# An attention and MoE kernel on one core: where the last stores stand, which engine makes widths and biases, and a new instruction order

## The chip, the cores and the metric

The kernel runs on one core of a Trainium2 chip. A core has engines with queues of their own: TensorE (PE, matmuls; PEld is its weight load), VectorE (DVE), ScalarE (ACT), GpSimd (POOL) and SyncE (SP), which here issues all DMAs. Each engine takes its instructions in order and waits on semaphores for the others. The metric is device microseconds (us) of one execution; the time of a kernel is the median of its runs.

## The reference

Attention over 4 batches, 8 heads, 768 positions and 64 columns, in which a query sees only keys of its own hash bucket, and then a gated two-matrix layer ("MoE") on the result. Cut to what matters:

```python
q_bucket = sum(((q @ proj) > 0) * 2**arange(6));  k_bucket = the same of k
scores = where(q_bucket[..., None] == k_bucket[:, :, None], q @ k.T / 8, -1e9)
attn = exp(scores - max(scores));  attn = attn / (sum(attn) + 1e-9)
x = (attn @ v), heads side by side: 3072 x 512
out = ((x @ w_a) * (x @ w_b)) @ w_out        # 512 -> 1536 -> 512, all float32
```

## The kernel before

Float32 operands are split into a high and a low float16 part, and a product is three float16 matmuls (high-high, high-low, low-high). The kernel is a list of some 3,600 small steps; `op(engine, duration, function, key, reads, writes, alt=...)` adds one. A step may name other engines in `alt`. The list ORDER, found by a search and written out as numbers, fixes the order of all steps: `issue` goes through it, an entry x above 9999 takes alternative x // 10000 of step x % 10000, and a negative entry -n puts n filler matmuls (`warm`) on PE. Every engine's queue follows ORDER.

Work is tiled by batch b, chunk c of 256 positions (three a batch) and half (two pairs of heads), so there are 24 units of 8 score tiles each, 192 in all, numbered u in a unit. The first two units use float32 for their attention (`by_pe`).

- Head: `kprep`, `qprep` and `vload` load q, k and v (SP), find a scale (`magnitude`, `scale_of`: a matmul of PE spreads a maximum, DVE makes the power of two), split (`split`, `vsplit`: high part on ACT, DVE or POOL, low part by `low` on DVE) and transpose. `proj_parts` scales the projection `pj`; its maximum goes through the matmul `ps_proj`. `w_group` and `wo_group` split the weights in the same way.
- A score tile, `qtile`: PE makes the scores `s` (one of two banks of PSUM), DVE the row maximum `mx` (L1164), then `width` (L1173, DVE), the 128x1 factor of the exponential, and `bias` (L1180 on ACT, or L1186 on DVE), then ACT the exponential `e` (L1196), which frees the bank. `e` is cast to float16 (`a`, high), subtracted (`a`, low, POOL or DVE, L1219 or L1223), transposed by a DMA and multiplied with `vv` on PE (`av`, L1238).
- `moe`: per chunk, 12 slices f of the hidden size: PE `ab` (L1389), ACT `a`, DVE `g`, its high part, POOL its low part g1 (L1432), PE `o` (L1442). At the end of a chunk two tiles of 128 rows are evicted to `ob` (two buffers, tag `ob`) and stored by SP (L1510). In the very last chunk (`alone`) the second tile is evicted in two halves of its columns, one by ACT (L1471) and one by DVE (L1478), into one `ob` buffer.

In ORDER the store of tile (b 3, c 1, u 1) is step 3355. Its eviction is step 3354, whose place is some 80 entries ahead of the end; step 3355 itself is the last entry of all, behind 3614, the store of the last tile:

```python
    3604, 3600, 3605, 3606, 3607, 3608, 13610, 3611, 3612, 3613, 3614, 3355,
```

(3607 and 3608 are the last `o` matmuls of tiles 0 and 1, 13610 the eviction of tile 0 on DVE, 3611 its store, 3612 and 3613 the halves of tile 1.)

Of the kernel before, what the change touches and what calls it, by code (L numbers as in the profile page):

```python
# [12 lines left out]
F32 = mybir.dt.float32  # L13
# [3 lines left out]
AF = mybir.ActivationFunctionType  # L17
ALU = mybir.AluOpType
# [3 lines left out]
P = 128  # L22
NB, NH, S, D = 4, 8, 768, 64
# [52 lines left out]
def constants():  # L76
# [1531 lines left out]
```

## Time and profile before

| what | us |
|---|---|
| three runs | 891.8, 887.73, 893.16; median 891.8 |
| the profiled execution | 890.85 |
| its span, first to last instruction | 889.1 |
| busy in it: PE, DVE, ACT, POOL | 858.7, 634.0, 507.4, 431.1 |
| mean granted clock of PE | 0.995 of full speed |

The profile is of one execution. Busy times are those of instructions, not of waits; a busy PE isn't PE at its peak, since matmuls are pipelined. "issue" is idle time that nothing in the profile explains. A wait is put down to the semaphore that came last.

### The profile page before, as it was taken

The page shows a single profiled execution, that of the slowest core. Times are in us where ns is not written, and L with a number is a line of the kernel's source. Part 1 is how long each engine was busy: PE and PEld are TensorE (multiplying, and loading weights), DVE is VectorE, ACT ScalarE, POOL GpSimd, SP SyncE. Part 2 cuts the span into 40 slices and gives each one's busy share as a digit, 9 for nine tenths or more (in the row PEclk, how much of TensorE's full clock was granted, in tenths as well). Part 3 has the DMA queues.
Part 4 walks back from the last instruction along what each step waited for, and adds up shares of the span by engine and source line. Part 5 has one row for each costly group of instructions (what it writes and reads, how often), then busy time and mean ns, then how long its engine had stood idle before and what let it go on. Part 6 is the DMA issues. An engine that isn't in the chain of part 4 may idle for free.

```text
span 889.1 us, 22944 instructions
## 1 busy us (share of the span) xinstructions
PE 858.7 (97%) x9255; PEld 654.1 (74%) x9255; DVE 634.0 (71%) x1390; ACT 507.4 (57%) x988; POOL 431.1 (48%) x399
## 2 busy tenths in 40 slices
PE   6799999999999999999999999999999999999996
PEld 4578766777777777777777777777777777777774
DVE  6999999987867777867765675787877568653211
ACT  6899998856566555564443445544674454432211
POOL 4558886645466456655353344542256542232111
PEclk9999999999999999999999999999999999999998
DMA  9968999999999899999857768988988975644000
GB/s 324 335 129 242 189 230 205 197 179 200 201 189 171 150 170 182 191 171 193 160 114 114 122 136 155 186 159 165 207 166 153 178 121 114 94 93 84 11 3 36
DMA packets 416986, 142.60 MB, mean 160 GB/s; under 512 B 388592, under 2 KB 409200, under 8 KB 416880
## 3 DMA queue, kind: packets, MB, share of 16 engines
q1 hardware_dynamic: 416880, 141.14, 82.0%
q8 instruction: 72, 1.18, 0.6%
q14 instruction: 34, 0.28, 0.1%
HBM read 37.82 MB, written 6.29 MB: 50 GB/s over the span
## 4 chain that ended last, share of the span: by engine, by line
PE 81%; DVE 10%; DMA 4%; issue 2%; ACT 1%; POOL 1%; SPq 1%; DVEq 0%; ACTq 0%; POOLq 0%
PE ab L1389 39%; PE o L1442 19%; PE s L1150 11%; PE av L1238 9%; DVE mx L1164 2%; DVE wab L573 1%; DMA vr<-in_v_dram 1%; DVE wmx L642 1%; DMA at<-a 1%; DVE vv L855 1%; DVE a L1223 1%; DMA qTA_q<-marked 1%; ACT e L1196 1%; DMA raw_w<-in_moe_w_a_dram 1%; DMA raw_wo<-in_moe_w_out_dram 0%
## 5 line engine op out<-in xcount | busy, mean ns | idle before, releaser
L1389 PE MATMUL ab<-xT,wab 128*128 128x256 f16 x3456 | 409.4, 272 | 1.9 <-DVE g L1412 1.9
L1389 PEld LDWEIGHTS <-wab 128*128 128x128 f16 x3456 | 332.9, 98 | 59.6 <-issue 3.1
L1432 POOL TENSOR_TENSOR g<-g,g 128x256 f16<-128x256 f32 x144 | 113.0, 785 | 308.7 <-ACT g L1420 135.2
L1196 ACT ACTIVATE e<-s,bias,width 128x768 f32<-128x768 f32 x192 | 189.9, 989 | 73.3 <-DVE bias L1186 57.9
L1164 DVE TENSOR_REDUCE mx<-s 128x1 f32<-128x768 f32 x192 | 182.0, 950 | 36.0 <-PE s L1150 35.3
L1442 PE MATMUL o<-wo,g 128*128 128x512 f16 x864 | 207.6, 379 | 0.0
L1219 POOL TENSOR_TENSOR a<-e,a 128x768 f16<-128x768 f32 x102 | 169.7, 1665 | 63.2 <-DVE a L1207 24.4
L1404 ACT ACTIVATE a<-ab,wcut 128x256 f32<-128x256 f32 x144 | 67.9, 471 | 183.1 <-PE ab L1389 182.0
L1412 DVE SCALAR_TENSOR_TENSOR g<-ab,wlow,a 128x256 f32<-128x256 f32 x132 | 63.5, 481 | 136.7 <-ACT a L1404 115.6
L1442 PEld LDWEIGHTS <-g 128*128 128x128 f16 x864 | 81.8, 98 | 77.1
L1238 PEld LDWEIGHTS <-at 128*128 128x128 f16 x3168 | 110.8, 98 | 16.6 <-DMA at<-a 3.3
L1238 PE MATMUL av<-vv,at 128*128 128x64 f16 x3168 | 116.2, 193 | 0.3 <-DMA at<-a 0.2
L1150 PE MATMUL s<-kTA_k,qTA_q 128*128 128x384 f16 x384 | 93.8, 326 | 5.2 <-ACT e L1196 3.3
L1150 PE MATMUL s<-kTB_k,qTB_q 128*128 128x384 f16 x384 | 93.7, 326 | 0.0
L1223 DVE TENSOR_TENSOR a<-e,a 128x768 f16<-128x768 f32 x74 | 80.2, 1086 | 9.3 <-POOL a L1209 6.0
L1208 ACT CAST a<-e 128x768 f16<-128x768 f32 x78 | 64.3, 828 | 7.9 <-issue 4.0
L1180 ACT ACTIVATE bias<-mx,width 128x1 f32<-128x1 f32 x89 | 25.8, 291 | 55.8 <-DVE width L1173 55.6
L1150 PEld LDWEIGHTS <-qTB_q 128*128 128x128 f16 x384 | 37.5, 98 | 24.9
L1209 POOL CAST a<-e 128x768 f16<-128x768 f32 x43 | 38.9, 907 | 23.2 <-ACT e L1196 15.6
L1420 ACT CAST g<-g 128x256 f16<-128x256 f32 x73 | 29.3, 402 | 36.1 <-DVE g L1412 22.5
L1150 PEld LDWEIGHTS <-qTA_q 128*128 128x128 f16 x384 | 34.0, 98 | 20.1 <-issue 7.5
L1173 DVE TENSOR_SCALAR width<-mx,qsig_q 128x1 f32<-128x1 f32 x192 | 39.5, 209 | 3.6
(165 smaller groups left out, 800.2 us busy)
## 6 DMA issues: line engine op xcount, KB each, us to landing
rk_k<-in_k_dram SPq DMA_DIRECT2D x16, 384.0 KB, 4.3
rq_q<-in_q_dram SPq DMA_DIRECT2D x12, 512.0 KB, 4.7
vr<-in_v_dram SPq DMA_DIRECT2D x16, 384.0 KB, 4.3
raw_w<-in_moe_w_b_dram SPq DMA_DIRECT2D x12, 512.0 KB, 6.9
raw_w<-in_moe_w_a_dram SPq DMA_DIRECT2D x12, 512.0 KB, 7.7
raw_wo<-in_moe_w_out_dram SPq DMA_DIRECT2D x12, 512.0 KB, 5.2
out_dram<-ob SPq DMA_DIRECT2D x24, 256.0 KB, 3.0
at<-a SPq DMA_TRANSPOSE x176, 4.0
```

The lines of the kernel that those rows point to most:

```text
L1150: nc.tensor.matmul(ps.t[:, jj, :HALF], lhsT=x.t[:, uq, :], rhs=y.t[:, h * NT + jj * 3 : h * NT + jj * 3 + 3, :].rearrange("p t x -> p (t x)"),
L1164: lambda: nc.vector.tensor_reduce(out=mx.t[:, u : u + 1], in_=halves(ps.t), axis=AX.XY, op=ALU.max, negate=True),
L1196: lambda: nc.scalar.activation(flat2(e.t), halves(ps.t), AF.Exp, bias=bias.t[:, u : u + 1], scale=width.t[:, u : u + 1], accum_out=sm.t[:, ...
L1208: ("ACT", 0.725, lambda: nc.scalar.copy(out=a2.t[:, 0], in_=e.t), False),
L1219: lambda: nc.gpsimd.tensor_tensor(out=a2.t[:, 1], in0=e.t, in1=a2.t[:, 0], op=ALU.subtract),
L1223: lambda: nc.vector.tensor_tensor(out=a2.t[:, 1], in0=e.t, in1=a2.t[:, 0], op=ALU.subtract), True,
L1238: nc.tensor.matmul(av.t[:, u, :], lhsT=at.t[:, a + kt, :], rhs=w.t[:, h, kt, x, :], start=i == 0, stop=i == 3 * NT - 1,)
L1389: nc.tensor.matmul(pl.t[:, m, :CH], lhsT=wt(m, wi, cc, f), rhs=xt.t[:, cc // 2, xi, cc % 2 * TPC : (cc % 2 + 1) * TPC, :], start=i == 0, s ...
L1404: lambda a=a, pl=pl, gr=gr: nc.scalar.activation(a.t, pl.t[:, 0, :CH], AF.Copy, scale=wcut[:, gr : gr + 1]),
L1412: lambda a=a, g32=g32, pl=pl, cut=cut: nc.vector.scalar_tensor_tensor(out=g32.t, in0=pl.t[:, 1, :CH], scalar=cut, in1=a.t, op0=ALU.mult, o ...
L1432: lambda g=g, g32=g32: nc.gpsimd.tensor_tensor(out=g[1].t, in0=g32.t, in1=g[0].t, op=ALU.subtract),
L1442: nc.tensor.matmul(po.t[:, u, :], lhsT=g[gi].t[:, us], rhs=wo[f // 2].t[:, f % 2, wi * DM : (wi + 1) * DM], start=f % per_q == 0 and i == ...
```

## The change

1. Widths may go to POOL (`wide`), biases too (`moved`), and low parts of q and k too (`low_too`, two instructions).
2. The halves of the last tile are evicted into two buffers of the tag `e` (`end_0`, `end_1`), and each half has a store of its own.
3. ORDER is another list. In it step 3355 stands right behind its eviction; the last two `o` groups are swapped; there are 16 more fillers (144 for 128); 51 widths, 25 biases and 2 low parts take POOL; among the first DMAs the two loads of `pj` stand ahead of `ident` and of the first q load.

```diff
 ORDER = [
...
-    3604, 3600, 3605, 3606, 3607, 3608, 13610, 3611, 3612, 3613, 3614, 3355,
+    3538, 3533, 3348, 3349, 3539, 3534, 3350, 3545, 3352, 3353, 13354, 3355, 3540, 3535, 3546, 3536, 3541, 3530, 3547,
...
+    3601, 3599, 3593, 3603, 3604, 3600, 3605, 3606, 3608, 3607, 3612, 3614, 13610, 3611, 3613, 3615,
 ]
...
+        def low_too():
+            nc.gpsimd.tensor_scalar(out=x, in0=x, scalar1=sc.t, scalar2=1.0, op0=ALU.mult, op1=ALU.mult)
+            nc.gpsimd.tensor_tensor(out=part(B, lo_at), in0=x, in1=part(B, hi_at), op=ALU.subtract)
+
+        op(
+            "DVE", -0.03 + 0.073 * n, low, key, r=[raw, *rtoks, (B, "hi")], w=[(B, "lo")],
+            sbuf=True, alt=[("POOL", 0.2 + 0.2 * n, low_too, False)],
         )
...
+        def wide(eng):
+            eng.tensor_scalar(
                 out=width.t[:, col], in0=mx.t[:, col], scalar1=NONE, scalar2=sig.t[:, hp : hp + 1], op0=ALU.is_lt, op1=ALU.mult
+            )
+        op(
+            "DVE", 0.13, lambda: wide(nc.vector), key - 0.5, r=[(mx, u), (sig, half)], w=[(width, u)],
+            alt=[("POOL", 0.17, lambda: wide(nc.gpsimd), False)],
+        )
+        def moved(eng):
+            eng.tensor_scalar(
+                out=bias.t[:, col], in0=mx.t[:, col], scalar1=width.t[:, col], scalar2=top, op0=ALU.mult, op1=ALU.add
+            )
...
+            alt=[("DVE", 0.15, lambda: moved(nc.vector), False), ("POOL", 0.17, lambda: moved(nc.gpsimd), False)],
         )
...
                 if alone and u == TPC - 1:
-                    hs = [slice(0, DM // 2), slice(DM // 2, DM)]
+                    ends = [buf("e", [P, S], F32, f"end_{x}", NE) for x in range(2)]
+                    cols = [slice(x * DM // 2, (x + 1) * DM // 2) for x in range(2)]
                     op(
                         "ACT", 0.36,
...
+                            ends[0].t[:, : DM // 2], po.t[:, u, cols[0]], AF.Copy, scale=osc.t
...
+                            out=ends[1].t[:, : DM // 2], in0=po.t[:, u, cols[1]], scalar1=osc.t, scalar2=None, op0=ALU.mult
...
+                    for x in range(2):
+                        op(
+                            "SP", DMA_ISSUE,
+                            lambda u=u, x=x: nc.sync.dma_start(
+                                out=out_v[b, c * TPC + u][:, cols[x]], in_=ends[x].t[:, : DM // 2]
+                            ),
+                            ke + 4, r=[ends[x]], w=[("out", b, c, u, x)], svc=0.8,
+                        )
+                    continue
```

## Rows read from the trace of the kernel before

**Rows 1.** busy time of the engines by stretch: start:end, length, each engine, PE's clock, DMA

```profile
0.00:25.00 25.00, 15.67 (x184) 11.46 (x184) 18.02 (x51) 17.90 (x22) 10.05 (x16) 1.00 0.92 324
25.00:150.00 125.00, 113.25 (x1188) 90.75 (x1188) 118.44 (x256) 115.64 (x190) 88.85 (x66) 0.99 0.94 221
150.00:880.00 730.00, 728.26 (x7881) 551.40 (x7879) 496.32 (x1082) 373.38 (x777) 332.15 (x318) 1.00 0.81 145
```

**Rows 2.** the same view, of the tile `warm` alone: length, PE busy

```profile
0.00:150.00 150.00, 19.89 (x128) 0.99 0.93 238
```

**Rows 3.** timeline of the end: start, us, engine, line, operation, tiles, idle before it and releaser

```profile
877.48 4.05 PE L1442 MATMUL o<-wo,g 128*128 128x512 f16 x18
881.57 0.75 DVE L1492 TENSOR_SCALAR ob<-o,osc 128x512 f32<-128x512 f32 x1 [2.77 <-PE o L1442]
884.47 0.47 ACT L1471 ACTIVATE ob<-o,osc 128x256 f32<-128x256 f32 x1 [5.17 <-DMA out_dram<-ob]
884.97 0.48 DVE L1478 TENSOR_SCALAR ob<-o,osc 128x256 f32<-128x256 f32 x1 [2.65 <-ACT ob L1471]
885.48 0.81 SPq L1510 DMA_DIRECT2D out_dram<-ob  x2
```

**Rows 4.** the line of the output stores: issue time of one, first and last start, landing

```profile
L1510 SPq DMA_DIRECT2D out_dram<-ob x24: 332/876/1516, 210.7 to 885.9; - x24
DMA to landing us min/median/max: 2.0/3.0/4.2
```

**Rows 5.** the chain that ended last, at the end: start, us, what

```profile
882.35 2.01 DMA out_dram<-ob
```

**Rows 6.** groups by line and form (busy, mean ns), and the smallest POOL operation (min/median/max ns)

```profile
L1173 DVE TENSOR_SCALAR width<-mx,qsig_q 128x1 f32<-128x1 f32 x192 | 39.5, 209 | 3.6
L1186 DVE TENSOR_SCALAR bias<-mx,width 128x1 f32<-128x1 f32 x103 | 21.7, 210 | 2.3 <-DVE width L1173 0.2
L1219 POOL TENSOR_TENSOR a<-e,a 128x768 f16<-128x768 f32 x102 | 169.7, 1665 | 63.2 <-DVE a L1207 24.4 <-ACT a L1208 23.0 <-issue 8.2
L1093 POOL TENSOR_SCALAR qsig_q<-kinv,qmx_q x11: 258/265/700, 25.8 to 617.0; 128x2 f32<-128x2 f32 x11
```

**Rows 7.** who waited for whom: us in all, times, longest

```profile
ACT e L1196 <- DVE bias L1186: 57.9, 37, 4.8
PE s L1150 <- ACT e L1196: 3.3, 5, 1.2
```

**Rows 8.** timeline, the line of v's low part, and a stretch, in the head

```profile
31.86 2.98 POOL L669 TENSOR_TENSOR wab<-wab 128x1024 f16<-128x1024 f32 x1
32.78 2.88 DVE L855 SCALAR_TENSOR_TENSOR vv<-vr,vsc,vv 128x768 f16<-128x768 f32 x1
L855 DVE SCALAR_TENSOR_TENSOR vv<-vr,vsc,vv x16: 998/1010/2876, 15.7 to 664.1; 128x768 f16<-128x768 f32 x16
39.98 1.00 PE L1117 MATMUL et<-ident,e 128*128 128x128 f32 x6 [2.76 <-ACT e L1196]
42.00:44.00 2.00, 2.00 (x12) 1.75 (x11) 2.00 (x4) 1.30 (x2) 2.00 (x2) 0.50 0.75 143
```

**Rows 9.** timeline of the first 15 us

```profile
1.75 0.43 SPq L1038 DMA_DIRECT2D rq_q<-in_q_dram  x1
2.22 1.36 SPq L432 DMA_DIRECT2D pj<-in_proj_dram  x2
6.99 0.16 DVE L493 TENSOR_REDUCE pmx<-pj 128x1 f32<-128x6 f32 x1 [1.39 <-DMA pj<-in_proj_dram]
7.70 0.90 POOL L974 TENSOR_SCALAR nB_k<-rk_k,ks_k 128x768 f16<-128x768 f32 x1 [6.09 <-DVE ks_k L480]
8.75 1.00 DVE L990 SCALAR_TENSOR_TENSOR nB_k<-rk_k,ks_k,nB_k 128x768 f16<-128x768 f32 x1
9.67 1.10 DVE L502 TENSOR_SCALAR pjk<-pj,psc 128x6 f16<-128x6 f32 x1
12.88 1.42 ACT L944 COPY kTB_k<-t_k_DVE 128x1536 f16<-128x1536 f16 x1
```

More of the change, by code (lines that the diff above doesn't have):

```diff
@@ L988, in split, with low @@
         )
-        def low(eng):
-            eng.scalar_tensor_tensor(
+        def low():
+            nc.vector.scalar_tensor_tensor(
                 out=part(B, lo_at), in0=x, scalar=sc.t, in1=part(B, hi_at), op0=ALU.mult, op1=ALU.subtract
             )
-        op(
-            "DVE", -0.03 + 0.073 * n, lambda: low(nc.vector), key, r=[raw, *rtoks, (B, "hi")], w=[(B, "lo")],
-            sbuf=True,
+        def low_too():
+            nc.gpsimd.tensor_scalar(out=x, in0=x, scalar1=sc.t, scalar2=1.0, op0=ALU.mult, op1=ALU.mult)
+            nc.gpsimd.tensor_tensor(out=part(B, lo_at), in0=x, in1=part(B, hi_at), op=ALU.subtract)
+        op(
+            "DVE", -0.03 + 0.073 * n, low, key, r=[raw, *rtoks, (B, "hi")], w=[(B, "lo")],
+            sbuf=True, alt=[("POOL", 0.2 + 0.2 * n, low_too, False)],
         )
@@ L1170, in qtile @@
         col = slice(u, u + 1)
-        op(
-            "DVE", 0.13,
-            lambda: nc.vector.tensor_scalar(
-                out=width.t[:, col], in0=mx.t[:, col], scalar1=NONE, scalar2=sig.t[:, hp : hp + 1], op0=ALU.is_lt, op1=ALU.mult
-            ),
-            key - 0.5, r=[(mx, u), (sig, half)], w=[(width, u)],
-        )
+        def wide(eng):
+            eng.tensor_scalar(
+                out=width.t[:, col], in0=mx.t[:, col], scalar1=NONE, scalar2=sig.t[:, hp : hp + 1], op0=ALU.is_lt, op1=ALU.mult
+            )
+        op(
+            "DVE", 0.13, lambda: wide(nc.vector), key - 0.5, r=[(mx, u), (sig, half)], w=[(width, u)],
+            alt=[("POOL", 0.17, lambda: wide(nc.gpsimd), False)],
+        )
+        def moved(eng):
+            eng.tensor_scalar(
+                out=bias.t[:, col], in0=mx.t[:, col], scalar1=width.t[:, col], scalar2=top, op0=ALU.mult, op1=ALU.add
+            )
         op(
@@ L1183, in qtile @@
             key - 0.5, r=[(mx, u), (width, u)], w=[(bias, u)],
-            alt=[(
-                "DVE", 0.15,
-                lambda: nc.vector.tensor_scalar(
-                    out=bias.t[:, col], in0=mx.t[:, col], scalar1=width.t[:, col], scalar2=top,
-                    op0=ALU.mult, op1=ALU.add,
-                ),
-                False,
-            )],
+            alt=[("DVE", 0.15, lambda: moved(nc.vector), False), ("POOL", 0.17, lambda: moved(nc.gpsimd), False)],
         )
@@ L1467, in moe @@
                 if alone and u == TPC - 1:
-                    hs = [slice(0, DM // 2), slice(DM // 2, DM)]
+                    ends = [buf("e", [P, S], F32, f"end_{x}", NE) for x in range(2)]
+                    cols = [slice(x * DM // 2, (x + 1) * DM // 2) for x in range(2)]
                     op(
                         "ACT", 0.36,
-                        lambda u=u, osc=osc, po=po, h=hs[0]: nc.scalar.activation(
-                            ob[u].t[:, h], po.t[:, u, h], AF.Copy, scale=osc.t
+                        lambda u=u, osc=osc, po=po: nc.scalar.activation(
+                            ends[0].t[:, : DM // 2], po.t[:, u, cols[0]], AF.Copy, scale=osc.t
                         ),
-                        ke - 8, r=[(po, u), osc], w=[(ob[u], 0)],
+                        ke - 8, r=[(po, u), osc], w=[ends[0]],
                     )
@@ L1477, in moe @@
                         "DVE", 0.34,
-                        lambda u=u, osc=osc, po=po, h=hs[1]: nc.vector.tensor_scalar(
-                            out=ob[u].t[:, h], in0=po.t[:, u, h], scalar1=osc.t, scalar2=None, op0=ALU.mult
+                        lambda u=u, osc=osc, po=po: nc.vector.tensor_scalar(
+                            out=ends[1].t[:, : DM // 2], in0=po.t[:, u, cols[1]], scalar1=osc.t, scalar2=None, op0=ALU.mult
                         ),
-                        ke - 8, r=[(po, u), osc], w=[(ob[u], 1)],
+                        ke - 8, r=[(po, u), osc], w=[ends[1]],
                     )
-                elif fq == 0 or whole:
+                    for x in range(2):
[7 more added lines that the diff above has]
+                    continue
+                if fq == 0 or whole:
                     op(
```

378 rows, old and new, of the table ORDER are left out of this document.

## The prediction

> **What bounds the kernel now.** I read the busy time by stretches first. Between 150 and 880 us TensorE (PE) is busy 728.26 of 730 us at a granted clock of 1.00; before 150 us it is busy 15.67 of 25 and 113.25 of 125, so 21.1 us stand idle there, and in that second stretch VectorE (DVE) has 118.44 and ScalarE (ACT) 115.64 of 125 us [rows 1]. Of PE's work in the first 150 us, 19.89 us are the filler matmuls `warm`, which compute nothing [rows 2]. So there are three parts: a head of 150 us bound by DVE, ACT and loads, a middle in which PE has no room, and a tail. In the middle no cheaper DVE or ACT instruction can gain anything (1.7 us of idle time in 730); it can only lose. That most edits of this change lie there is the main fact of this prediction.
>
> The tail I read from the timeline and the chain that ended last. PE's last 18 output matmuls end at 877.48 + 4.05 = 881.53 us. DVE evicts the first tile (0.75), its store is issued at 882.35, and then ACT does not begin the second tile's half until 884.47: it sat idle 5.17 us, ended by a DMA of `out_dram<-ob`. DVE's half follows (0.48), and two stores are issued from 885.48 on, the last at 885.9 [rows 3 to 5]. The chain shows the 2.01 us of the first store inside the path [rows 5]. The code says why: in the old ORDER the store of tile (3,1,1), op 3355, is the very last entry, so its `ob` buffer is never given back, and the last tile has to take the buffer of (3,2,0) once that store has landed. Behind the evictions, 889.1 - 885.9 = 3.2 us pass for landing and closing.
>
> **The change, part by part.**
>
> Tail. Op 3355 now stands right behind its eviction, some 40 us before the end, where SyncE (SP) has little else to issue. The last tile's halves get buffers of the tag `e`, long free by then, and a store each. In the new order the PE does tile 1's last three matmuls before tile 0's, so tile 1 is complete 4.05/18 x 3 = 0.68 us before 881.53, at about 880.9. ACT's half is done at 880.9 + 0.5 = 881.4, its store is out by 881.8. DVE evicts tile 0 from 881.57 to 882.32 as before, and its own half only after that: 882.33 + 0.48 = 882.82. The last store is issued at 882.85 instead of 885.9: 3.05 us less. The extra issue costs at least 0.33 us of SP [rows 4] and is hidden: the three issues stand 0.5 us or more apart. A store of 128 KB on its own has no row; stores of 256 KB landed in 2.0 to 4.2 us, median 3.0 [rows 4], and the one in the chain in 2.01. I take the same 3.2 us behind the last issue, since half the bytes come behind a store that has 0.5 us of lead. If it lands only after 4.2, about 2 us more than the chain's, the gain is 1.1; 0.2 us more than I take would be the most it can give back. **Tail: -3.0 us (-1.1 to -3.3).**
>
> Widths and biases. Counting the op numbers of the new ORDER, 51 of 192 widths and 25 of 192 biases run on GpSimd (POOL). DVE loses 51 x 0.209 and 12 x 0.210 = 13.2 us, ACT loses 13 biases [rows 6]. POOL has no such row: its nearest is `qsig`, 128x2, 0.258 least, 0.265 median, 0.700 most [rows 6], so 76 x 0.27 = 20 us, up to 53. I take 0.27, since that row has the same operation and one column more. POOL has 332 of 730 us in the middle [rows 1], so the load fits. Only 7 widths and 4 biases lie in batch 0, that is in the head; the rest lie where PE is full. Value there: 0, covered by PE's own work. What it costs without that cover: the width leads to the bias, the bias to the exponential `e`, and `e` frees the score bank that PE writes next. The waits show `e` waiting for a bias 37 times, 57.9 us in all, but PE waiting for `e` only 5 times, 3.3 us in all [rows 7]. So a step that is 0.06 us longer is lost in the slack of most tiles. Behind a waiting width on POOL stand the next subtraction, its transposing DMA and PE's `av`.
>
> A rule against this edit: once, at 31.86, a POOL subtraction ran 2.98 us and a DVE low part of v beside it 2.88, where that line's median is 1.010 [rows 8]. The Trainium skill (GPSIMD Engine Reference, Specifications) says that GpSimd shares its SBUF interfaces with VectorE and contends with VectorE instructions of two SBUF inputs; the trace agrees in that pair. By the rows of the moved instructions the edit costs 0, as summed here; by that rule the 20 us of new POOL work could hold DVE for as long, and if a tenth of it reached PE the time would be 2 us longer, 890. I keep 0.
>
> Two of the 28 low parts (q of batch 1, k of batch 3) go to POOL in two instructions. A POOL conversion of 768 columns is 0.90 [rows 9], a subtraction of 768 is 1.67 [rows 6]: 2.6 us for k, 4/3 of it, 3.4, for q. Both lie in the middle; 0 while POOL's idle time covers them, at most 6 us if all of it came onto the path.
>
> New order, head. SP issues both `pj` loads straight behind the first k load; `ident` and the q load, which stood ahead of them (q at 1.75), are issued the 1.36 us of those two later [rows 9]. Before, DVE sat behind `pj` until 6.99 and GpSimd got the k scale only at 7.70 after 6.09 idle us [rows 9]. Now `pj` comes early, `ident` lands about 1.3 later, and PE has `ps_proj` ahead of `ps_k`; the k scale should come about 1 us sooner. Against that q's scale comes up to 1 us later (its load was awaited), and the four `pjk`/`pjq` instructions now stand ahead of k's low part on DVE: 8.75 before, now behind `pjk`'s 1.10 and three smaller ones, near 11 to 12 [rows 9]. The next reader, ACT's copy of k's transpose, began at 12.88, behind ACT's v sums, so some 1.9 us of this is covered. **First 25 us: +0.4 (-1 to +1.5).** Behind it, up to the end of batch 0, I counted DVE's work ahead of equal PE steps in both orders at the rows' durations: the new order has about 2 us less of DVE, 1 to 2 less of ACT and 3 to 4 more of POOL. DVE is 95% busy there [rows 1], so half of the 2 us may reach PE: **-0.9 (-2 to +1).** The filler grows from 128 to 144 matmuls, 16 x 19.89/128 = 2.5 us [rows 2]; they are put where PE would be idle: 0, or +2.5 if it isn't. **Head: -0.5 (-3 to +4).**
>
> Middle. A new order of some 3,600 steps can open or close gaps; there is 1.7 us to close. I take +0.3 (-1 to +6).
>
> Sum against the profiled execution (span 889.1, 890.85 with what lies around it): 890.85 - 3.0 - 0.5 + 0.3 = 887.65. The three runs have a median of 891.8, 0.95 above that execution. I forecast **888.0**: a third of that offset kept.
>
> **The rivals.**
>
> A. The head gains more. After the stretched pair at 31.86, PE stood 2.76 us for `e`, and for the two us from 42 the granted clock was 0.50, the 1.2 GHz level [rows 8]. If the new order keeps these two apart, the stall of 2.8 and about 1 us of half clock go too: 888.0 - 3.8 = 884.2, and with DVE's whole 2 us 883. Against it: the new lists still have a low part of v on DVE and a low part of W on POOL near the same scores.
>
> B. It ends on the other side: POOL becomes the late link. Of the 76 moved instructions 29 stand right behind a g1 subtraction, which waits for a MoE matmul group, and others behind `a` subtractions of 1.67 [rows 6]. Place: 150 to 800 us. The price for one is up to 1.67 plus what the subtraction itself waits, less the slack. If a quarter of the 76 lose 0.5 us of PE time, 9.5 us: 888.0 + 9.5 = 897.5; it is slower than before from 3.8 us on, 8 tiles at 0.5. For it: POOL is in order, PE has no idle time to give, and the stretched pair [rows 8] shows POOL late when DVE works beside it. Against it: PE's few waits for `e` [rows 7].
>
> C. The tail does not do what it says: the last halves still wait for something, a landing of 4.2 or a later DVE half. Then -1.1 instead of -3.0: 889.9.
>
> **How the numbers follow.** Forecast (884.5 to 891.5) 0.60; A 0.13; B 0.20; C 0.07. The range has to leave out 2 in 10: below, it reaches A's 883; above, half of B: 895. A time within 1% (882.9 to 900.7 against 891.8) is what a measurement of this kernel can hardly tell from no change. Faster by over 1% needs 5 us beyond the forecast, more than A gives: 0.05. Slower by over 1% needs 12.7 us lost, the far end of B: 0.05. Within 1%: 0.90.
>
> **What would show it.** Tail: ACT's half at about 880.9 with no DMA ahead of it, the last store issued some 1.3 us behind PE's last matmul. Middle: PE busy again 728 of 730, PE's waits for `e` near 3 us; if they rise past 7, or an `s` matmul waits behind a POOL width, B holds. Widths on POOL at 0.27 or less. Head: idle PE time before 150 us near 21; 17 or less is A. I am wrong if the last store's issue comes over 2 us behind PE's end, or if the middle loses over 4 us.

## The result, and the profile after

The changed kernel takes 884.87 us (median of 9 runs, 882.83 to 886.4) against 893.16 for the kernel before on the same chip (887.73 to 894.09): a ratio of 0.9917, 95% interval 0.9898 to 0.9936. That is 8.3 us less there; a second measurement gave 885.79 against 892.49, 6.7 us less. The forecast was 888.0 with a range of 883 to 895, so the time lies inside the range, 3.1 us below the forecast and near rival A's 884.2.

The profiled executions are 890.85 us (before) and 886.4 (after), 4.45 apart. The first lies below its kernel's median, the second is the longest of its nine runs. So the pair of profiles shows little more than half of what the medians show, and where the rest lies had to be found by runs.

Busy time of the engines by stretch, kernel after (answers [rows 1]: start:end, length, PE, PEld, DVE, ACT, POOL, PE's granted clock, DMA share, GB/s):

```profile
0.00:25.00 25.00, 15.65 (x185) 12.04 (x186) 15.95 (x47) 18.05 (x22) 10.25 (x17) 1.00 0.91 333
25.00:150.00 125.00, 116.48 (x1204) 93.01 (x1202) 116.50 (x258) 116.40 (x187) 97.62 (x73) 0.97 0.96 221
150.00:875.00 725.00, 724.43 (x7862) 550.41 (x7860) 482.33 (x1019) 370.91 (x764) 361.36 (x389) 1.00 0.80 146
```

The same view, of the tile `warm` alone (answers [rows 2]):

```profile
0.00:150.00 150.00, 21.24 (x144) 0.98 0.95 240
```

PE stands idle 9.35 + 8.52 = 17.9 us before 150 us (21.1 before). But 1.35 of the 3.2 us won are fillers, and PE's clock was at its low level for longer. Busy time by stretch, before (first line) and after (second):

```profile
40.60:44.00 3.40, 3.40 (x19) 2.76 (x18) 3.40 (x6) 2.55 (x4) 3.06 (x2) 0.50 0.57 136
50.90:57.70 6.80, 6.80 (x30) 5.03 (x30) 2.82 (x9) 4.95 (x10) 5.27 (x4) 0.50 0.75 235
```

That is half of 6.8 - 3.4, so 1.7 us of PE time. In this pair of executions the head gave nothing that shows (3.2 - 1.35 - 1.7). The middle is as full as before: 0.6 idle of 725, where it was 1.7 of 730.

Timeline of the end, kernel after (answers [rows 3]: start, us, engine, line, operation, tiles, idle before it and releaser):

```profile
875.85 4.05 PE L1450 MATMUL o<-wo,g 128*128 128x512 f16 x18
...
879.94 0.47 ACT L1480 ACTIVATE end<-o,osc 128x256 f32<-128x256 f32 x1 [2.33 <-PE o L1450]
880.44 0.33 SPq L1495 DMA_DIRECT2D out_dram<-end  x1
880.45 0.75 DVE L1510 TENSOR_SCALAR ob<-o,osc 128x512 f32<-128x512 f32 x1 [3.33 <-ACT end L1480]
881.11 0.48 DVE L1487 TENSOR_SCALAR end<-o,osc 128x256 f32<-128x256 f32 x1
...
881.65 0.38 SPq L1495 DMA_DIRECT2D out_dram<-end  x1
```

The DMA that held ACT for 5.17 us in [rows 3] is gone. PE's end is 875.85 + 4.05 = 879.90, the span's end 884.6: 4.70 us behind PE, where it was 889.1 - 881.53 = 7.57. The tail gave 2.87 of the 4.45; 1.1 of the rest is the middle's idle time, and that is no more than executions of one kernel differ (after_again, the changed kernel once more, has 1.9 us idle there).

The moved instructions, kernel after (answers [rows 6]; groups by line: busy us, mean ns | idle before them and its releasers):

```profile
L1179 POOL TENSOR_SCALAR width<-mx,qsig_q 128x1 f32<-128x1 f32 x51 | 21.4, 419 | 54.0 <-DVE mx L1170 52.8 <-DVE pw_v L472 0.2
L1189 POOL TENSOR_SCALAR bias<-mx,width 128x1 f32<-128x1 f32 x25 | 7.6, 305 | 16.0 <-DVE width L1179 12.2 <-ACT g L1428 2.0
```

The line of the widths there (min/median/max ns, first and last start):

```profile
L1179 DVE TENSOR_SCALAR width<-mx,qsig_q x141: 193/214/215, 35.5 to 793.7; 128x1 f32<-128x1 f32 x141
L1179 POOL TENSOR_SCALAR width<-mx,qsig_q x51: 294/301/1362, 28.4 to 796.3; 128x1 f32<-128x1 f32 x51
```

The waits that answer [rows 7] (us in all, times, longest):

```profile
ACT e L1204 <- DVE bias L1189: 60.5, 31, 4.6
PE s L1156 <- ACT e L1204: 1.0, 3, 0.4
PE ab L1397 <- DVE g L1420: 1.3, 2, 1.0
```

A width on POOL costs 0.30 in the median and 0.42 in the mean, against 0.21 on DVE, and yet PE waits for `e` less than before: 1.0 us, 3 times.

### The profile page after: what moved, and what is told of

Same layout as the page of the kernel before. It is cut to its first block, busy times and chain, and to the rows that moved or that the text cites. A ratio compares the mean times of both kernels' runs of the same rounds, so it can differ in the third digit from the quotient of the medians.

```text
span 884.6 us, 22994 instructions
## 1 busy us (share of the span) xinstructions
PE 861.5 (97%) x9271; PEld 657.9 (74%) x9271; DVE 616.4 (70%) x1325; ACT 506.7 (57%) x974; POOL 470.4 (53%) x480
## 4 chain that ended last, share of the span: by engine, by line
PE 82%; DVE 4%; DMA 3%; ACT 2%; POOL 1%; issue 1%; SPq 0%; DVEq 0%; ACTq 0%; POOLq 0%
PE ab L1397 39%; PE o L1450 20%; PE s L1156 12%; PE av L1246 9%; DMA at<-a 2%; DVE mx L1170 1%; DMA kTB_k<-nB_k 1%; POOL a L1227 1%; ACT e L1204 1%; DVE wo_y L574 0%; PE av L1137 0%; PE b_k L897 0%; DVE g L1420 0%; PE b_q L897 0%; DVE a L1231 0%
## 5 line engine op out<-in xcount | busy, mean ns | idle before, releaser
L1227 POOL TENSOR_TENSOR a<-e,a 128x768 f16<-128x768 f32 x102 | 171.9, 1691 | 55.9 <-DVE a L1215 23.3
L1231 DVE TENSOR_TENSOR a<-e,a 128x768 f16<-128x768 f32 x74 | 77.3, 1049 | 5.8 <-ACT a L1216 3.7
L1216 ACT CAST a<-e 128x768 f16<-128x768 f32 x82 | 67.5, 826 | 6.9 <-DMA at<-a 5.5
L1217 POOL CAST a<-e 128x768 f16<-128x768 f32 x48 | 43.0, 897 | 30.7 <-ACT e L1204 18.7
L1195 ACT ACTIVATE bias<-mx,width 128x1 f32<-128x1 f32 x76 | 22.1, 291 | 53.3 <-DVE width L1179 36.8
L1179 POOL TENSOR_SCALAR width<-mx,qsig_q 128x1 f32<-128x1 f32 x51 | 21.4, 419 | 54.0 <-DVE mx L1170 52.8
L1432 DVE TENSOR_REDUCE g<-g 128x256 f16<-128x256 f32 x78 | 32.2, 413 | 8.0 <-PE o L1450 5.9
```

Source lines behind the costliest of these rows:

```text
L1216: ("ACT", 0.725, lambda: nc.scalar.copy(out=a2.t[:, 0], in_=e.t), False),
L1227: lambda: nc.gpsimd.tensor_tensor(out=a2.t[:, 1], in0=e.t, in1=a2.t[:, 0], op=ALU.subtract),
L1231: lambda: nc.vector.tensor_tensor(out=a2.t[:, 1], in0=e.t, in1=a2.t[:, 0], op=ALU.subtract), True,
```

## The experiments

All times are medians on the chip. The kernel before, measured again beside each group, took 892.84, 892.49 and 892.17 us.

One thing about the change must be known first. The new ORDER does more than re-order and move 78 steps to POOL: read number by number, it gives another engine to 272 further steps, by alternatives that the kernel before had too (DVE casts 46 of the tiles `a` instead of 55, for example). The list of the change doesn't name them. "The new order" below means the order together with these 272.

### The tail by itself, and the new order without it

**tail_only**: the old order with the new tail. Entries of ORDER, cut to those that move:

```diff
+    3355,   (behind steps 3353 and 3354)
...
-    3607, 3608, 13610, 3611, 3612, 3613, 3614, 3355,
+    3608, 3607, 3612, 3614, 13610, 3611, 3613, 3615,
```

> The kernel before with the tail of the change alone: step 3355 moved behind its eviction, the halves of the last tile in two end buffers with a store each, the last two o groups swapped; all other steps in the old order, no width, bias or low part on GpSimd. Theory T (the tail is 2.8 us of the gain, as the two profiles show: 7.5 us from PE's end to the end of the span before, 4.7 after): about 2.8 us under the kernel before, ratio 0.997; PE ends where it did, 4.7 us of span follow. Rival O (most of the gain is the new order and its engines): T's tail appears too, but the time stays over 4 us above the changed kernel. Rival N (the tail is hidden or given back): ratio 1.000.

**no_tail**: the changed kernel with the old tail (one `ob` buffer for the halves, step 3355 last).

> The changed kernel with the tail undone: old halves in one ob buffer, one store, step 3355 last of all, the last two o groups in the old places. Theory T: loses the 2.8 us of the tail, so about 887.7 where the changed kernel has 884.9; if the medians (8.3 us apart) hold, the rest of 5.5 us below the kernel before is the new order. Rival: if it comes out at the kernel before, the tail was everything.

tail_only: 889.0 us (886.45 to 891.24), ratio 0.9958 (0.9943 to 0.9972), 3.8 us below the kernel before, with T's 2.8 inside the interval. no_tail: 888.72, ratio 0.9955 (0.9943 to 0.9967), 2.9 to 3.9 above the changed kernel. So tail and order are worth some 3 to 4 us each and add up; neither needs the other. In tail_only's profile PE ends at 879.05 + 4.05 = 883.10 and the span at 887.8: 4.70 us, as in the changed kernel. In no_tail's the wait for the store is back, and 886.9 - (875.32 + 4.05) = 7.5 us follow PE's end (timeline):

```profile
882.30 0.47 ACT L1479 ACTIVATE ob<-o,osc 128x256 f32<-128x256 f32 x1 [5.23 <-DMA out_dram<-ob]
```

### The moved widths and biases

**no_pool**: the changed kernel with all 51 widths, 25 biases and 2 low parts on DVE. This isn't quite where they were: 13 of the 25 biases ran on ACT in the kernel before. Entries of ORDER, cut:

```diff
-    20032, 258, 76, 10074, 10085, 255,
+    20032, 258, 76, 10074, 85, 255,
...
-    383, 95, 159, -6, 20102, 10330,
+    383, 95, 159, -6, 10102, 10330,
...
```

> The changed kernel, its order of steps kept, but all 51 widths and 25 biases that run on GpSimd put back on VectorE, and the 2 low parts too. Theory P0 (the moves are worth nothing, since PE has no idle time from 150 us on): within 1 us of the changed kernel. Rival P+ (the moves carry the order's gain by relieving VectorE): 2 to 5 us slower than the changed kernel, with PE waiting more for e. Rival P- (they cost, as the mean width on GpSimd took 0.419 us for 0.213 on VectorE): 1 to 3 us faster.

**old_pool**: tail_only with the same 78 steps sent to POOL, their places in the old order kept.

> The tail of the change and the old order of steps, but the 51 widths, 25 biases and 2 low parts that the change puts on GpSimd put there too. The run without these moves in the new order was 4 us slower than the changed kernel and equal to the old order with the new tail (889.0 both). Theory M (the moves themselves relieve VectorE where it is late for PE): about 885, like the changed kernel. Rival J (moves and order are worth something only together, since the order was searched with them): 888 to 892, no better than 889.

no_pool: 889.0 us (0.9953, 0.9941 to 0.9966), 3 to 4 above the changed kernel: P0 missed, P+ has the time. old_pool: 899.34 us (1.008, 1.0057 to 1.0104), 10.3 above tail_only: far from M, and 7 above what J allowed. The waits of old_pool, and one of no_pool (us in all, times, longest):

```profile
ACT bias L1195 <- POOL width L1179: 24.3, 16, 3.9
ACT e L1204 <- POOL bias L1189: 20.5, 15, 2.9
PE s L1156 <- ACT e L1204: 8.1, 12, 1.3
PE ab L1397 <- DVE g L1420: 3.7, 4, 1.4
```

```profile
PE ab L1397 <- DVE g L1420: 3.2, 6, 1.3
```

In old_pool the chain of rival B is there: a late width on POOL, a late bias, a late `e`, and PE waits for `e` 12 times and 8.1 us, where the changed kernel has 3 times and 1.0. Of the 8.1 us, 4.8 lie behind 150 us, where tail_only has 0.8; `ab` waits there 2.5 us for `g` (1.1 in tail_only). So B's chain is the largest single part of the loss, not all of it. PE's idle time in old_pool from 150 us on, by stretches:

```profile
150.00:300.00 150.00, 146.88 (x1661) 110.50 (x1658) 117.48 (x262) 97.02 (x193) 95.41 (x98) 1.00 1.01 185
300.00:600.00 300.00, 295.67 (x3257) 223.56 (x3256) 205.03 (x426) 151.95 (x318) 160.33 (x172) 1.00 0.85 155
600.00:890.00 290.00, 287.57 (x2983) 218.16 (x2982) 164.37 (x343) 122.54 (x257) 111.25 (x120) 1.00 0.61 112
```

3.1 + 4.3 + 2.4 = 9.9 us, against 1.7 in [rows 1]. no_pool shows the reverse: the new order without the moves leaves DVE late, though not for `e` as P+ said: PE waits for `e` 0.8 us, but `ab` for `g` 6 times instead of 2. From 150 to 879 us PE is idle 3.5 us (0.6 in the changed kernel), and 2.3 of them lie in one place. Busy time of PE there, no_pool and the changed kernel:

```profile
200.00:265.00 65.00, 62.68 (x681) 1.00 1.06 198
200.00:265.00 65.00, 65.00 (x722) 1.00 1.08 208
```

How much of this is the 13 biases that came from ACT (13 x 0.21 = 2.7 us more on DVE) wasn't separated. The moves are worth neither +10 nor -4 us by themselves; they fit the order that they stand in.

### Where in the order the rest of the gain lies

**new_head** and **old_head** cut both orders at the first score of unit (0,2,1), step 899, some 155 us into the run, and join them crosswise, both with the new tail. **after_again** is the changed kernel once more beside them.

```
new_head: the new order up to  885, 10879, 10886, 448,    then what is left, in the old order
old_head: the old order up to  1070, 10879, 10886, 448,   then what is left, in the new order
```

> The changed kernel's order up to the first score of unit (0,2,1), about 150 us into the run, and behind it the old order with the new tail; widths and biases on GpSimd only in that head (11 of 76). Theory mid (the 4 us lie behind 150 us, where the middle of the profiles lost 3.5 to 4.1 us of PE time in the new order, 5.1 to 6.0 in the old): 888 to 889. Rival head (they lie in the head: fewer stalls and low clock): 885 to 886.

> The reverse: the old order up to the first score of unit (0,2,1), behind it the changed kernel's order with its 65 moved widths and biases and its tail. Theory mid: 885 to 886. Rival head: 888 to 889. If both hybrids lie halfway, each part holds about 2 us.

> The changed kernel once more, unchanged, in one call with the three below, so that differences of one us can be read. Expected 884.9 as before (ratio 0.992 to the kernel before).

| first 155 us | rest | kernel | us | ratio to before |
|---|---|---|---|---|
| old | old | tail_only | 889.0 | 0.9958 (0.9943 to 0.9972) |
| old | new | old_head | 890.49 | 0.997 (0.9954 to 0.9987) |
| new | old | new_head | 886.1 | 0.9932 (0.9912 to 0.9953) |
| new | new | after_again | 885.79 | 0.9922 (0.9901 to 0.9942) |

The new head is worth 2.9 us with the old rest and 4.7 with the new; the new rest is worth +1.5 and -0.3, which the intervals don't tell from nothing. The first of the two differences has intervals that overlap a little; those of the second don't. So rival head holds in both. new_head is as quick as the changed kernel with 8 of the moves alone (5 widths and 3 biases; the text before the run counted 11): behind 155 us the 70 others, the new order and its engines together bring nothing that can be measured.

Across the profiles the head's gain is plainer than in the one pair. PE's idle time before 150 us is 19.9 to 21.1 us in the three with the old head (before, tail_only, old_head) and 15.8 to 17.9 in the six with the new one (after, after_again, no_tail, no_pool, new_head, head_dve), about 1 us of it taken by fillers.

**new_45**: the new order only for its first 210 entries (to the score of tile 4 of the first unit, 45 us in the changed kernel), then the old order, with the new tail.

> The new order for its first 210 steps (to the score of tile 4 of the first unit, 45 us in the changed kernel), then the old order, with the new tail. Theory (the head's gain is that the stall of PE at 37 us, 2.9 us, and the half clock behind it are gone): all of the head's gain is here, 885.5 to 886.5. Rival (the gain is made between 45 and 150 us, where the old order waits some 0.5 to 1.2 us each at 85, 115, 127, 135 and 148 us): 888.5 to 889.5.

**head_dve**: the changed kernel with the head's 5 widths and 3 biases on DVE again.

> The changed kernel with the 5 widths and 3 biases that it gives to POOL in the first 150 us back on DVE; the 68 others of the moves stay on POOL. If the head's gain comes from relieving DVE there: 3 us or so higher, near 889, PE's idle time in the first 150 us near 45 us instead of 43 to 45. If it comes from the order alone: as the changed kernel, 885 to 886.5. That leaves the whole price of putting all of them back (3 to 4 us) to the middle.

new_45: 886.2 us (0.993, 0.9904 to 0.9957). head_dve: 884.94 us (0.9911, 0.9894 to 0.9928). So POOL's widths in the head give nothing (PE is idle 15.8 us before 150 us in head_dve; the 43 to 45 us of the text before the run are no idle time that a view shows). By the medians what the head gains is made in the first 45 us; but new_45's six runs reach from 883.57 to 890.69, and its interval overlaps with tail_only's (0.9943 to 0.9972), so this is likely and not shown. What differs there between the old head (tail_only) and the new (new_45), in their timelines:

```profile
32.09 2.99 POOL L669 TENSOR_TENSOR wab<-wab 128x1024 f16<-128x1024 f32 x1
33.02 2.88 DVE L855 SCALAR_TENSOR_TENSOR vv<-vr,vsc,vv 128x768 f16<-128x768 f32 x1
...
40.21 1.54 PE L1117 MATMUL et<-ident,e 128*128 128x128 f32 x6 [2.89 <-ACT e L1196]
```

```profile
38.20 0.87 PE L1122 MATMUL et<-ident,e 128*128 128x128 f32 x6 [0.20 <-ACT e L1203]
```

The stretched pair and PE's stall of [rows 8] stand in tail_only too (2.99, 2.88 and 2.89 us). In new_45 the two stand apart (1.00 and 2.14), and the same `et` waits 0.20 and runs at full clock, 0.87 for 1.54. That is the stall of rival A, gone from its place. The low clock isn't gone with it; it comes later and for longer (busy time by stretch, new_45):

```profile
45.00:52.00 7.00, 5.87 (x83) 4.80 (x82) 6.83 (x23) 5.65 (x11) 6.58 (x7) 1.00 1.04 158
52.00:62.20 10.20, 8.93 (x38) 6.66 (x38) 6.93 (x17) 8.31 (x11) 5.63 (x6) 0.50 0.40 92
```

Of the six profiles with the new head only new_head's has no stretch at 0.50 in the head. So A's half clock isn't what the new head gains.

### The stretched pair by itself

**pair_apart**: tail_only with one step moved, the low part of `vv` behind the second of the two widths that follow it. Entries of ORDER, cut:

```diff
-    80, -3, 71, 291, 311, 100,
+    80, -3, 291, 311, 100,
...
-    103, 93, 160, 161,
+    103, 93, 71, 160, 161,
```

> The old order with the new tail (889.0 in its own run), with one step moved: the low part of vv on DVE (2.88 us in the profile of before, beside POOL's subtraction of the weights with 2.98) goes behind the two row maxima and widths that stood behind it. Theory (rival A of the forecast: this stretched pair holds DVE's maxima, PE then stands for 2.9 us at 37 us with et waiting for e, and PE's clock falls to 0.5 behind that): the subtraction on POOL takes about 2.1, the maxima start near 34.3 instead of 35.8, PE's stall falls from 3.05 to about 1.5 us or less and the clock at 40 to 44 us with it; time 1.5 to 3 us lower, 886 to 887.5. Rival, the head has other waits right behind it (weights' maxima on DVE, the transposed k by DMA): the stall moves and the time stays 888.5 to 889.5.

Its profiled execution took 887.61 us. At the pair it does what the theory says (timeline):

```profile
33.35 2.13 POOL L669 TENSOR_TENSOR wab<-wab 128x1024 f16<-128x1024 f32 x1
...
34.41 0.96 DVE L1169 TENSOR_REDUCE mx<-s 128x1 f32<-128x768 f32 x1 [0.43 <-PE s L1155]
...
35.54 1.01 DVE L855 SCALAR_TENSOR_TENSOR vv<-vr,vsc,vv 128x768 f16<-128x768 f32 x1
...
37.70 0.88 PE L1122 MATMUL et<-ident,e 128*128 128x128 f32 x6 [0.26 <-ACT e L1203]
...
43.21 0.23 PE L589 MATMUL ps_w<-ident,wmx 128*128 128x128 bf16 x1 [1.25 <-DVE wmx L654]
```

Busy time by stretch there:

```profile
40.00:44.00 4.00, 2.38 (x40) 1.95 (x38) 3.40 (x10) 2.94 (x4) 3.29 (x3) 0.95 1.11 304
44.00:48.00 4.00, 4.00 (x25) 3.78 (x24) 3.96 (x7) 2.85 (x3) 3.85 (x4) 0.50 0.91 207
```

Apart, the two take 2.13 and 1.01 instead of 2.99 and 2.88, and `et` waits 0.26. PE idles a little later instead (1.25 for `ps_w`, 1.6 of the four us from 40), and then runs at 0.50, the 1.2 GHz level. But the median of its 12 runs is 893.67 us, 1.0007 (0.9986 to 1.0028) of the kernel before and 4.7 above tail_only: the forecast of this experiment, 886 to 887.5, is missed by 6 us, and so is the rival's 888.5 to 889.5, though the stall moves as it said.

What differs from run to run is PE's mean granted clock, which each run lists. Runs at 0.999 and 0.995 took 886.04 and 887.61; the other ten had 0.986 to 0.994 and took 892.5 to 896.51. From the lowest clock to the highest, 0.013 x 893 = 11.6 us of PE time are missing, and the times (895.6 and 895.75 against 886.04) differ by 9.6. The clock isn't all of it: 0.994 took 892.64, 5 us more than 0.995. The same reckoning, (1 - clock) x 890 in the mean of the runs, is an estimate of the PE time that the clock took:

| kernel | runs | median us | mean clock | (1 - clock) x 890, us |
|---|---|---|---|---|
| before (three groups) | 46 | 892.4 | 0.9954 | 4.1 |
| tail_only | 7 | 889.0 | 0.9966 | 3.0 |
| pair_apart | 12 | 893.67 | 0.9902 | 8.7 |
| new_45 | 6 | 886.2 | 0.9962 | 3.4 |
| changed kernel, both times | 15 | 885.4 | 0.9972 | 2.5 |
| fill_k2 (below) | 6 | 886.01 | 0.9993 | 0.6 |

The mean clock counts time in which PE has nothing left to do. In the profile of before it is 0.50 again from 883.7 us to the end, 2 us behind PE's last matmul (busy time by stretch):

```profile
883.70:889.10 5.40, 0.00 (x0) 0.00 (x0) 0.48 (x1) 0.47 (x1) 0.00 (x0) 0.50 0.29 109
```

These 5.4 us make 2.7 in the last column, where the kernel's runs have 4.1 in the mean. In the profiles with the new tail the same part is 0 to 1.3 us. So the rows with the new tail can be compared to about 1 us, and the row of before can't be set against them.

By this estimate pair_apart without its lost clock is at 885 us (893.67 - 8.7), tail_only at 886, new_45 at 882.8: taking the pair apart would gain something like 1 us where the clock holds, and lose 8.7 - 3.0 = 5.7 by the clock. The gain isn't shown: tail_only's two runs at 1.000 took 886.45 and 888.68, and pair_apart's one at 0.999 886.04. Where in the ten slow runs the clock was low isn't known: the profiled execution isn't one of them. Why new_45, which has the same stall removed, keeps a mean of 0.9962 is open too.

### Fillers against the low clock

**fill_k2**: the changed kernel with 18 more fillers ahead of step 154, where PE idles 2.35 us for the DMA of k's transpose.

```diff
-    392, 294, 154, 553,
+    392, 294, -18, 154, 553,
```

> The changed kernel with 18 more filler matmuls ahead of the marks of batch 0's third k pair (step 154), where PE stood 2.35 us for a DMA in the profile and the granted clock was 0.50 to 0.71 for some 7 us behind that. Theory C (the clock fell because PE stood still; the low clock cost 3 us of real work): the clock stays 1.00 there and the time falls by 2 to 3 us against the changed kernel, or by less if not all executions have the dip. Rival D (the dip costs nothing since VectorE and ScalarE bound the head): same time within 1 us, though the clock stays up. If the fillers are in the way (the DMA landing earlier in most executions): up to 2 us slower.

The changed kernel at that place (timeline):

```profile
50.08 0.76 PE L892 MATMUL b_k<-pjk,kTB_k 128*128 128x6 f16 x24 [2.35 <-DMA kTB_k<-nB_k]
```

Busy time by stretch there:

```profile
48.00:50.00 2.00, 0.00 (x0) 0.00 (x0) 1.42 (x3) 1.18 (x3) 1.90 (x3) 1.00 0.93 207
50.00:52.00 2.00, 1.92 (x31) 1.93 (x32) 1.66 (x5) 1.97 (x3) 1.57 (x2) 0.71 0.61 121
52.00:54.00 2.00, 2.00 (x10) 1.61 (x10) 0.00 (x0) 1.97 (x6) 2.00 (x2) 0.50 0.53 127
```

fill_k2 at the same place:

```profile
50.00:54.00 4.00, 3.66 (x40) 2.87 (x37) 3.93 (x11) 3.93 (x8) 2.42 (x3) 1.00 0.57 103
54.00:58.00 4.00, 3.88 (x29) 2.80 (x28) 3.77 (x12) 3.78 (x6) 3.76 (x4) 1.00 0.99 313
```

The fall of the clock is gone, in the mean of the runs too (0.9993), and the time is 886.01 us (0.9929, 0.9916 to 0.9942): not lower, so theory C missed and rival D has the time. By the table 1.9 us of clock came back. 18 fillers are 18 x 21.24/144 = 2.7 us of PE work, some of it in the idle time. But in the profile the head did get shorter: the first exponential of unit (0,2,1) starts at 162.57 us, and at 164.87 in the changed kernel. As much is lost again behind it, as idle time of PE (fill_k2):

```profile
300.00:600.00 300.00, 297.52 (x3279) 1.00 0.89 157
```

That is 2.5 us idle, 0.4 in the changed kernel's profile (1.3 in after_again's), and PE ends at 880.13 us, no earlier than there (879.90). This is one execution of each; why the middle takes the gain is open.

### Why the last halves waited, and a faster end

**own_banks**: the changed kernel, with tile 1 of the last chunk summed in a PSUM tile of its own, and each of the two last tiles evicted whole, tile 1 by ACT, tile 0 by DVE.

```diff
+                po1 = buf("ab", [P, 2, CH], F32, f"o1_{n}", 1, pp) if alone else None
...
-                    w=[(po, u) for u in us_],
+                    w=[(po1 if po1 is not None and u else po, u) for u in us_],
...
-                            ends[0].t[:, : DM // 2], po.t[:, u, cols[0]], AF.Copy, scale=osc.t
+                            end.t[:, :DM], po1.t[:].rearrange("p a b -> p (a b)"), AF.Copy, scale=osc.t
```

> The changed kernel, but in the last chunk the output of tile 1 is summed in a PSUM tile of its own (the bank of the tag ab, free there), and each of the last two tiles is evicted whole: tile 1, whose last matmuls go first, by ACT, tile 0 by DVE, one store each (one store fewer). Theory (in the changed kernel ACT's half of tile 1 waits for PE's very last matmul, and DVE's eviction for ACT's half, because both tiles are parts of one PSUM tile): ACT starts some 0.65 us before PE's last matmul ends and takes 0.68, DVE starts at PE's end and takes 0.75, the last store is issued about 0.8 us behind PE's end (1.75 in the changed kernel), PE's end to the end of the span falls from 4.71 to about 3.8 us, and the time is 0.9 us below the changed kernel's (884.9 against its 885.8). Rival 1, the engines wait for PE to be done, whatever the tile: ACT and DVE start together at PE's end; the last store would be as early, but ACT's start says so. Rival 2, two readers of PSUM follow each other whatever the tile: DVE starts when ACT ends, and the tail stays at 4.5 or more.

Timeline of its end; PE's last matmul ends at 877.58 + 4.05 = 881.63, the span at 885.4:

```profile
877.58 4.05 PE L1451 MATMUL o<-wo,g 128*128 128x512 f16 x18
...
881.02 0.69 ACT L1482 ACTIVATE end<-o,osc 128x512 f32<-128x512 f32 x1 [1.68 <-PE o L1451]
881.67 0.75 DVE L1502 TENSOR_SCALAR ob<-o,osc 128x512 f32<-128x512 f32 x1 [2.82 <-PE o L1451]
...
882.45 0.33 SPq L1520 DMA_DIRECT2D out_dram<-ob  x1
```

ACT starts 0.61 us before PE's end, DVE 0.04 behind it, and the last store is issued 0.82 behind PE's end instead of 1.75. The tail is 3.77 us for 4.70. Rival 1 falls by the 0.61 us. Rival 2 falls too, if narrowly: DVE starts 0.04 us ahead of ACT's end, where in the changed kernel it started 0.04 behind it. So it was the shared PSUM tile that made ACT wait for tile 0's matmuls and DVE for ACT's half. These waits are in the program, not in the chip: the Trainium skill (PSUM — Partial Sum Buffer, "PSUM bank collisions raise a hardware error") asks that two engines be kept apart only within one bank; here ACT reads one bank for 0.61 us while PE still writes the other, so the trace agrees. The median is 884.41 us (0.9908, 0.9888 to 0.9927), the lowest here; the 0.9 us don't stand clear of the changed kernel's 884.87 and 885.79, whose intervals overlap with it.

## Why the prediction was right, and where it wasn't

**Tail (-3.0): right in size, one step wrong.** Measured 2.87. Moving step 3355 freed the buffer, as worked out, and no DMA stands ahead of ACT's half. The step "ACT's half is done at 880.9 + 0.5 = 881.4" failed: tile 1 was complete 0.68 us before PE's end, but its reader waited for tile 0's matmuls too, being in the same PSUM tile, and DVE then waited for ACT. The last store came 1.75 us behind PE's end, not 1.32; 0.2 us came back behind it, where 884.6 - 881.65 = 2.95 passed instead of 3.2. So the swap of the two groups of `o` bought nothing here; own_banks shows the 0.9 us that were to be had in the trace.

**Widths and biases (0): right as a sum, at a wrong price, and for a reason that holds against the kernel before alone.** The price of one was put at 0.27, from the 128x2 `qsig`; the widths took 0.301 in the median and 0.419 in the mean, so 51 and 25 of them cost 21.4 + 7.6 = 29.0 us, not 20. In the changed kernel it cost nothing, since PE's waits for `e` stayed low. "A step that is 0.06 us longer is lost in the slack" holds for the order they were placed in alone: the same steps in the old order cost 10.3 us. And "in the middle no cheaper DVE or ACT instruction can gain anything" fails inside the new order: with the 78 steps on DVE, PE idles 3.5 us behind 150 us instead of 0.6, and the time is 3 to 4 us longer (no_pool). The two come to 0 against the old order, as new_head shows, which has the old order behind 155 us and is as quick. The prediction took order and moves as two terms; they are one. The rule weighed there (the Trainium skill, GPSIMD Engine Reference, Specifications), with the tenth that was assumed to reach PE, would have made it 890; the changed kernel doesn't show that loss. head_dve, with 8 of the moves undone, is as quick as the changed kernel.

**Rival B (897.5): did not happen, but its price was real.** old_pool is 10.3 us above tail_only, with B's own chain as the largest part. The forecast gave it 0.20 on the argument that POOL is in order and PE has no room. The two kernels with the same 78 moves differ in the order and in the engines of the 272 other steps; that it is the place of each step in its queue which decides is argued from the waits, not tried step by step. The prediction looked at neither.

**Head (-0.5, -3 to +4): the term that was mis-sized.** Measured -2.9 and -4.7 by the two crossings (the second lies outside the term's range), and -2.8 for the first 45 us alone. It was summed as a 25 us part (+0.4) and an amount of DVE work (-0.9). The first part came to about +1: the first exponential starts at 29.1 and 28.9 us in the changed kernel's profiles, at 27.9 to 28.2 with the old head. The second was too small: PE's idle time before 150 us fell by 3 to 4 us, while the moved steps hardly matter: with the 8 back on DVE the time is the same (head_dve). One stall of 2.8 us is seen to go, the one that the prediction had as rival A with 0.13. It did not look whether the new order keeps the pair apart, though ORDER says so: on POOL the high part of k (step 150) stands ahead of the low part of W (257) in the new list and behind it in the old one, so that the low part of `vv` (71) no longer meets 257 (1.00 and 2.13 us in the profile after). That this stall is what the head gains is not shown: pair_apart takes it away alone and is slower, and A's other part, the half clock, is longer after the change (6.8 us for 3.4). What in the head's order makes the gain stays open. The result lies inside the forecast case (884.5 to 891.5); that it is also near A's 884.2 doesn't make A right.

**What the sum stood on.** It started from an execution of 890.85 us and kept a third of the offset to the median. The kernel before has a median of 892.4 over 46 runs, so the forecast's 888.0 stood for a gain of 2.85 from 890.85, where the gain between medians is 6.7 to 8.3. The low start and the small gain cancel in part, and that is luck: the distance of 3.1 us to the result hides part of the head's error.

**Middle (+0.3): right within the noise.** -0.3 and +1.5 by the crossings. **Fillers (0 or +2.5)**: by the profile 1.35 us more of them stood in the head; not tried apart. **Rival C (889.9)** fell: the halves did wait for something, but for each other, and that cost 0.4.

**What would show it.** The widths were above 0.27; the last store lay under 2 us behind PE's end; idle time before 150 us was 17.9, between "near 21" and A's 17. In that execution the clock and the fillers took the difference back; only many runs, or the idle time of many profiles, show the gain.

## What to carry to other kernels

The same moves to another engine can cost 10 us, nothing, or be needed: judge them together with the order, not as a term of their own, and look at what stands ahead of each step in that engine's queue. When two big SBUF operations of DVE and POOL stand side by side ahead of a row maximum, look whether the other order parts them; but don't expect the time to follow, since here the stall and the low clock came back elsewhere. Where two engines read the two halves of one PSUM tile at the end of a kernel, give each half a tile of its own (0.9 us in the trace here, not clear of noise in the time); and take the time before from many runs, since one profile can stand 2 us off.

## What the runs showed of the hardware that was not expected

- A one-column `tensor_scalar` on POOL: 0.301 us in the median, 1.362 the longest, mean 0.419, against 0.214 on DVE.
- Side by side, a POOL subtraction of 1024 columns and a DVE operation of two SBUF inputs took 2.99 and 2.88 us; one after the other 2.13 and 1.01 (pair_apart). The Trainium skill (GPSIMD Engine Reference, Specifications) names this contention; the size is this case's.
- PE idle for some 2 us (48 to 50, kernel after) was followed by granted clocks of 0.71 and 0.50, the 1.2 GHz level; with fillers in that gap the clock stayed at 1.00.
- The granted clock falls to 0.50 behind PE's last matmul too (883.7 to 889.1 us, kernel before), so the mean clock of a run counts time that costs nothing.
- One step moved on DVE changed the mean clock of whole runs from 0.9966 (tail_only) to 0.9902 (pair_apart), with the kernel before at 0.9955 beside both, and the time by 4.7 us. Over pair_apart's twelve runs the time fell as the clock rose (correlation -0.91); over the 46 of the kernel before much less so (-0.48). What lowers the clock in one run and not in the next is open.
